# A small GpSimd copy ahead of the first weight load is taken out of a fused attention and feed-forward kernel

## The chip, the cores and the metric

The kernel runs on one core of one Trainium2 chip. The metric is device time in microseconds (us) of one execution, the median of several runs. Before the change it is 179.35 us (three runs, 179.14 to 179.39).

## What is computed

A gated linear recurrence over 768 positions, for 4 batches of 8 heads with head size 48, and behind it a two-layer network on all 3072 rows of 384 numbers:

```python
f = 1.0 / (1.0 + np.exp(-f_logit))
for t in range(S):
    state = f[:, :, t, :, None] * state + np.einsum('bhd,bhe->bhde', k[:, :, t], v[:, :, t])
    y[:, :, t] = np.einsum('bhd,bhde->bhe', q[:, :, t], state)
...
h = x @ w_in                      # 384 -> 2048
out = np.maximum(0.01 * h, h) @ w_out   # 2048 -> 384
```

All inputs and the output are float32.

## The kernel before

**Tiles.** The work is cut into twelve pairs, m = 0 to 11: pair m belongs to batch m % 4 and holds 2 x 128 positions of all 8 heads. The first four pairs are thus the first 256 positions of the four batches. For each pair four loads of 384 KB bring the gate input F, the keys K, the queries Q and the values V into float32 tiles `RAW["F"]`, `RAW["K"]`, `RAW["Q"]` and `RAW["V"]`, which have three slots each. Below, F1 means F of pair 1, the second pair, and so on. F1 goes to slot 1, F2, K2, Q2 and V2 to slot 2.

**A pair's way.** ScalarE takes exp(-F) and then ln(1 + .), which is minus the logarithm of the gate; a product with a triangular matrix on TensorE sums it along the positions; ScalarE turns the sums into decay factors; VectorE or GpSimd multiply K and Q with them (`scale`, L294). `state_pe` (L354) forms the pair's contribution to the state, `turn_pe` (L310) transposes the scaled K and Q, `score` (L324) multiplies them, `mask` (L333) masks, `mix` (L342, L345) forms y. `y_out`, `x_pe` (L381) and `x_out` move y, transposed, to `XT`. Then `up` (L392) multiplies with w_in, 8 groups of 6 matmuls for a pair; `up_act` (L408) is the leaky ReLU; `down` (L420) multiplies with w_out; `put` and `out_pair` bring the rows out. The first two pairs go through shorter code of the same kind with names that begin with `f_`.

**The weights.** w_in and w_out are float32 in memory and bf16 in their tiles. `load_w_in(0)` and `load_w_in(1)` (L246) bring one half each, 768 KB as stored in the tile; `up` groups 0 to 3 need the first half, groups 4 to 7 the second. Four `load_w_out` (L249) bring a quarter each. All six are issued by GpSimd and go through the queue q0; the loads of F, K, Q and V are issued by SyncE (L255) and go through q1. Both queues are served by the same 16 DMA engines.

**The order.** The whole program is one list written out by hand. Each engine does its part of the list in that order, and waits at the first instruction whose inputs aren't there; what stands behind it waits too. Around the change the list reads, cut to what matters (slot numbers are the last arguments of `load`):

```python
v_cast(G, 0, 0)            # GpSimd: V of pair 0 to bf16
load('F', 2, 2)            # SyncE
f_exp(1)                   # ScalarE: exp of F1, in place
touch('F', 1)              # GpSimd
load_w_in(0)               # GpSimd issues
load('V', 2, 2)            # SyncE
load_w_in(1)               # GpSimd issues
load('K', 2, 2)            # SyncE
v_cast(G, 1, 1)            # GpSimd: V of pair 1 to bf16
load_w_out(0, 1)           # GpSimd issues
put_state(0, 0)            # GpSimd
load('Q', 2, 2)            # SyncE
```

`touch` (L242) copies the last column of a slot of a raw tile to a tile `seen` of 128 x 1 that nothing reads. On ScalarE, `gate_exp(2)` (L259), the exp of F2, stands ahead of `x_out(A, 0, 0)` (L127), which gives the first `XT`, and ahead of `gate_ln(2)` (L262) and the first `up_act`. On VectorE, `v_cast(V, 2, 2)` of V2 stands ahead of `scale(V, 0, 2, 0, 1)` of K2 and `scale(V, 1, 2, 0, 1)` of Q2; `state_pe(1, 2, 1, 5)` on TensorE waits for the first two, `turn_pe(1, 1, 2)` for the third.

Of the kernel before, what the change touches and what calls it, by code (L numbers as in the profile page):

```python
# [15 lines left out]
def kernel(  # L16
# [122 lines left out]
    def f_exp(s, hh=None):  # L139
        t = part("F", s)[:, hd(hh)]  # L140
        A.activation(t, t, AF.Exp, scale=-1.0)  # L141
# [99 lines left out]
    def touch(name, s):  # L241
        G.tensor_copy(out=seen, in_=RAW[name][:, s, 96 * H - 1:96 * H])  # L242

    def load_w_in(x):
        c = 512 * sum(WP[:x])
        G.dma_start(out=WI[x], in_=moe_w_in.rearrange("(a p) n -> p a n", p=128)[:, :, c:c + 512 * WP[x]])  # L246
# [234 lines left out]
    f_back(0, 0, 5)  # L481
    v_turn(0, 6, 6 + 1)
    f_exp(1)
    touch('F', 1)
    load_w_in(0)
    idle_pe(1, 1)
    f_back_out(V, 0, 5)
# [753 lines left out]
```

## Time and profile before

| | |
|---|---|
| median of three runs | 179.35 us (179.14 to 179.39) |
| the profiled execution's own time | 179.37 us |
| span of its instructions | 177.7 us |
| TensorE busy | 167.7 us (94%) |
| ScalarE, VectorE, GpSimd busy | 114.0, 107.8, 70.8 us |
| granted TensorE clock | 0.999 |
| moved by DMA | 31.68 MB |

The span runs from the first to the last instruction of one profiled execution; 1.67 us of its time lie outside the span. In the profile PE is TensorE's matmuls, PEld its weight loads, DVE is VectorE, ACT ScalarE, POOL GpSimd, and SPq the queue of SyncE, which only issues transfers. In a timeline a row gives the start, the length, the engine, the line, the operation, out<-in, the shape and the count, and in brackets how long the engine had been idle and what ended that. A DMA row there is its issue and not the transfer; the time from issue to landing stands in other views. In the DMA view the rows of a queue give packets, megabytes, and the time that the packets took as a share of the 16 engines' time in that stretch, which can be above 100% since packets overlap.

### The profile page before, as it was taken

The numbers are of one execution on the slowest core, as the hardware profiler recorded it, in microseconds if no ns is written. First come the engines' busy times: TensorE is split into PE (matmuls) and PEld (weight loads), VectorE is DVE, ScalarE is ACT, GpSimd is POOL, SyncE is SP. The second block draws the span as 40 slices with busy tenths as digits, with TensorE's granted clock in tenths as the row PEclk, the third lists the DMA queues.
The fourth block names the chain that finished last, engine by engine and source line by source line (L and its number), as shares of the span: only waits on it lengthen the run. The fifth ranks groups of instructions, "written<-read, shape, count | busy, mean of one in ns | idle before, by whom it ended". The sixth has DMA issues, their size and how long they took to land.

```text
span 177.7 us, 4589 instructions
## 1 busy us (share of the span) xinstructions
PE 167.7 (94%) x1850; PEld 134.6 (76%) x1850; DVE 107.8 (61%) x219; ACT 114.0 (64%) x196; POOL 70.8 (40%) x114
## 2 busy tenths in 40 slices
PE   6987689999999999999999999999999999999992
PEld 4655579876795888697698688697796978778871
DVE  5298955357899996587979999393861302030110
ACT  3979459499589759779479598259162835336520
POOL 7369420037955540593666395756320000000000
PEclk9999999999999999999999999999999999999999
DMA  5999999999989999989999679988484000021315
GB/s 141 322 325 246 210 214 214 282 270 300 283 232 285 278 311 292 184 199 274 173 268 137 150 182 202 156 151 167 79 149 95 0 0 4 0 61 32 89 44 133
DMA packets 73764, 31.68 MB, mean 178 GB/s; under 512 B 69264, under 2 KB 72464, under 8 KB 73744
## 3 DMA queue, kind: packets, MB, share of 16 engines
q1 hardware_dynamic: 71680, 27.96, 67.1%
q0 software_dynamic: 1376, 3.15, 9.2%
q10 hardware_dynamic: 688, 0.30, 0.6%
q8 instruction: 14, 0.23, 0.5%
q14 instruction: 6, 0.05, 0.1%
HBM read 25.17 MB, written 4.72 MB: 168 GB/s over the span
## 4 chain that ended last, share of the span: by engine, by line
PE 81%; DMA 10%; SPq 3%; DVE 2%; ACT 1%; POOL 1%; issue 0%
PE ps L420 34%; PE ps L392 33%; DMA w_in<-in_moe_w_in_dram 7%; PE ps L324 3%; DMA rawF<-in_f_logit_dram 3%; SPq L255 2%; PE ps L345 2%; PE ps L354 2%; PE ps L342 2%; PE ps L425 1%; PE ps L310 1%; PE ps L381 1%; DVE kh L294 1%; PE ps L268 1%; POOL w_in L246 0%; ACT rawF L141 0%
## 5 line engine op out<-in xcount | busy, mean ns | idle before, releaser
L408 ACT ACTIVATE gT<-ps 128x512 bf16<-128x512 f32 x96 | 56.1, 599 | 33.0 <-PE ps L392 29.8
L392 PE MATMUL ps<-xT,w_in 128*128 128x256 bf16 x576 | 67.4, 273 | 2.2 <-DMA w_in<-in_moe_w_in_dram 2.2
L420 PE MATMUL ps<-w_out,gT 128*128 128x384 bf16 x368 | 65.9, 326 | 0.0
L392 PEld LDWEIGHTS <-w_in 128*128 128x128 bf16 x576 | 61.7, 113 | 3.6 <-DMA w_in<-in_moe_w_in_dram 2.4
L420 PEld LDWEIGHTS <-gT 128*128 128x128 bf16 x368 | 34.2, 98 | 20.2 <-issue 0.2
L333 DVE TENSOR_TENSOR wm<-ps,mask 128x512 bf16<-128x512 f32 x40 | 25.5, 684 | 9.7 <-PE ps L324 6.7
L129 DVE COPY osb<-ps 128x384 f32<-128x384 f32 x13 | 7.2, 555 | 29.6 <-PE ps L420 19.9
L236 POOL CAST sb<-sf 64x192 bf16<-64x192 f32 x40 | 15.3, 383 | 22.4 <-DVE sf L231 14.2
L302 DVE COPY vb<-vq 64x384 bf16<-64x384 bf16 x40 | 14.9, 372 | 1.0 <-PE ps L345 0.3
L361 DVE TENSOR_TENSOR sf<-sf,ps 64x192 f32<-64x192 f32 x32 | 11.2, 348 | 5.8 <-PE ps L354 4.8
L364 POOL TENSOR_TENSOR sf<-sf,aend 128x192 f32<-128x192 f32 x14 | 7.6, 542 | 13.7 <-DVE sf L361 12.4
L294 POOL TENSOR_TENSOR kh<-rawQ,aa 128x384 bf16<-128x384 f32 x12 | 11.7, 995 | 1.4 <-ACT aa L288 1.2
L294 DVE TENSOR_TENSOR kh<-rawK,em 128x384 bf16<-128x384 f32 x16 | 10.9, 721 | 1.7 <-DMA rawK<-in_k_dram 1.6
L127 ACT COPY osb<-ps 128x384 f32<-128x384 f32 (+1 forms) x12 | 5.3, 456 | 9.9 <-PE ps L420 6.8
L129 POOL CAST vq<-rawV 128x768 bf16<-128x768 f32 x10 | 8.9, 900 | 5.3 <-DMA rawV<-in_v_dram 5.3
L265 POOL TENSOR_TENSOR ls<-rawF 128x384 bf16<-128x384 f32 x8 | 8.5, 1068 | 6.1 <-ACT rawF L262 3.6
L127 ACT CAST xn<-ps 128x384 bf16<-128x384 f32 x15 | 7.1, 478 | 5.5 <-PE ps L345 5.4
L133 PE MATMUL ps<-fill 128*128 128x256 bf16 x38 | 7.9, 350 | 1.4 <-DVE fill L102 1.4
L285 ACT ACTIVATE em<-rawF 128x768 bf16<-128x768 f32 x10 | 8.5, 849 | 0.8 <-POOL rawF L279 0.6
L345 PE MATMUL ps<-vb,wm 128*128 128x48 bf16 x192 | 8.7, 183 | 0.0
L262 ACT ACTIVATE rawF<-rawF 128x768 f32<-128x768 f32 x10 | 8.4, 842 | 0.1
L259 ACT ACTIVATE rawF<-rawF 128x768 f32<-128x768 f32 x10 | 8.5, 846 | 0.0
(81 smaller groups left out, 175.6 us busy)
## 6 DMA issues: line engine op xcount, KB each, us to landing
rawK<-in_k_dram SPq DMA_DIRECT2D x12, 384.0 KB, 5.3
rawQ<-in_q_dram SPq DMA_DIRECT2D x12, 384.0 KB, 5.1
rawV<-in_v_dram SPq DMA_DIRECT2D x12, 384.0 KB, 5.0
rawF<-in_f_logit_dram SPq DMA_DIRECT2D x11, 384.0 KB, 5.0
out_dram<-osb SPq DMA_DIRECT2D x22, 192.0 KB, 3.1
w_in<-in_moe_w_in_dram POOLq DMA_DIRECT2D x2, 768.0 KB, 11.0
w_out<-in_moe_w_out_dram POOLq DMA_DIRECT2D x4, 384.0 KB, 14.7
kT<-kh SPq DMA_TRANSPOSE x14, 4.5
```

The source lines that it names most:

```text
L127: eng.copy(out=out, in_=in_)
L129: eng.tensor_copy(out=out, in_=in_)
L236: G.tensor_copy(out=SB[r, b, s, :, e * D:(e + 1) * D], in_=SF[r, b])
L259: A.activation(RAW["F"][:, s], RAW["F"][:, s], AF.Exp, scale=-1.0)
L294: eng.tensor_mul(o[:, :, j, :, 0:D], x[:, :, j], y[:, :, j])
L302: V.tensor_copy(out=VB[64 * j:64 * j + 64, vb, w, :], in_=VQ[64 * w:64 * w + 64, t, j * KD:(j + 1) * KD])
L333: V.tensor_mul(WM[:, wm, c].rearrange("p (i n) -> p i n", n=128), bank(bk)[:, c].rearrange("p (i n) -> p i n", n=128), masks(4 if hh is No ...
L345: nc.tensor.matmul(bank(bk)[:, h * D:(h + 1) * D], WM[:, wms[h % 2], 128 * (h // 2):128 * (h // 2) + 128], VB[:, vb, w, h * D:(h + 1) * D] ...
L361: V.tensor_add(SF[r, b], SF[r, b], pt[r, :, e * D:(e + 1) * D])
L392: nc.tensor.matmul(bank(bk)[:, i * 256:(i + 1) * 256].rearrange("p (w n) -> p w n", w=2), WQ[g // 2][:, f, :, g % 2 * 2 + i], XT[:, t, :, ...
L408: A.activation(GT[:, t, 2 * g:2 * g + 2, :].rearrange("p f n -> p (f n)"), bank(bk), AF.Prelu, alpha=0.01)
L420: nc.tensor.matmul(bank(bk)[:, 0:KD], GT[:, t, ff, 128 * w:128 * w + 128], WO[:, ff, :], start=(ff == 0), stop=(ff == NF - 1))
```

## The change

One line of the list goes; nothing else is edited.

```diff
     f_back(0, 0, 5)
     v_turn(0, 6, 6 + 1)
     f_exp(1)
-    touch('F', 1)
     load_w_in(0)
     idle_pe(1, 1)
```

On GpSimd, this is the place of the copy in the program as built, with the semaphores that each instruction waits for: DMAHW5 tells of the landing of V0, DMAHW6 of that of F1, and Activation counts ScalarE's instructions, here its exp of F1.

```order
 L129 CAST kh_71<-rawK_65 128x8x48 [waits DMAHW3_49]
 L129 CAST vq_72<-rawV_67 128x768 [waits DMAHW5_49]
-L242 COPY seen_117<-rawF_64 128x1 [waits DMAHW6_49,Activation_49]
 L246 DMA w_in0_83<-in_moe_w_in_dram 128x3x1024
 L246 DMA w_in1_84<-in_moe_w_in_dram 128x3x1024
```

The two loads wait for nothing of their own in either program, so they now stand right behind the cast of V0.

On SyncE, the later loads of F, K, Q and V have the same order, and some of their waits on a slot's earlier readers are written down elsewhere (Pool counts GpSimd's instructions). The rows are F3, F4, F5, K3, K4, Q3 and V3 in this order.

```order
 L255 DMA rawF_64<-in_f_logit_dram 128x8x96 [waits DMAHW5_49,Activation_49]
-L255 DMA rawF_64<-in_f_logit_dram 128x8x96 [waits DMAHW6_49,Activation_49,Pool_49]
+L255 DMA rawF_64<-in_f_logit_dram 128x8x96 [waits DMAHW6_49,Activation_49]
 L255 DMA rawF_64<-in_f_logit_dram 128x8x96 [waits DMAHW1_49,DMAHW7_49,DVE_49,Activation_49]
-L255 DMA rawK_65<-in_k_dram 128x8x96 [waits DMAHW0_49]
-L255 DMA rawK_65<-in_k_dram 128x8x96
+L255 DMA rawK_65<-in_k_dram 128x8x96 [waits DMAHW0_49,Pool_49]
+L255 DMA rawK_65<-in_k_dram 128x8x96 [waits Pool_49]
 L255 DMA rawQ_66<-in_q_dram 128x8x96 [waits DMAHW2_49]
-L255 DMA rawV_67<-in_v_dram 128x8x96 [waits DMAHW3_49]
+L255 DMA rawV_67<-in_v_dram 128x8x96 [waits DMAHW3_49,Pool_49]
```

F4's load no longer waits for the copy, and K3's, K4's and V3's now name the GpSimd casts that read their slots before, which the wait for the copy had covered. In the same way the first `f_state_pool` on GpSimd (L225) now names ScalarE beside VectorE.

## The prediction

> **What bounds the kernel now.** I read the chain of waits first, in shares and then in order of time:
>
> ```profile
> PE 81%; DMA 10%; SPq 3%; DVE 2%; ACT 1%; POOL 1%; issue 0%
> ...
> 10.36 0.85 ACT rawF L141
> ...
> 11.46 0.87 POOL w_in L246
> 12.33 12.79 DMA w_in<-in_moe_w_in_dram
> ...
> 25.16 1.50 PE ps L392 x12
> ```
>
> The end is set by TensorE, but the chain enters TensorE at 25.16 us, through the landing of the second half of w_in at 12.33 + 12.79 = 25.12. Behind that the table of stages (its length, then the busy time of PE, PEld, DVE, ACT and POOL, each with its instructions, the granted clock, the DMA share and GB/s) shows no room on TensorE: it is busy in 19.52 of the 20 us from 40 and in all of those from 60.
>
> ```profile
> 40.00:60.00 20.00, 19.52 (x252) 14.95 (x250) 17.67 (x35) 15.97 (x29) 14.74 (x21) 1.00 1.03 278
> 60.00:80.00 20.00, 20.00 (x211) 16.27 (x210) 16.09 (x33) 15.06 (x27) 9.18 (x14) 1.00 0.99 247
> ```
>
> So what TensorE wins at 25.16 it keeps, unless something else comes late. The timeline of TensorE shows what it waits for before:
>
> ```profile
> 18.83 0.51 PE L215 MATMUL ps<-vb,kb 128*128 128x96 bf16 x8
> 20.75 1.50 PE L392 MATMUL ps<-xT,w_in 128*128 128x256 bf16 x12 [1.41 <-DMA w_in<-in_moe_w_in_dram]
> ...
> 25.16 1.50 PE L392 MATMUL ps<-xT,w_in 128*128 128x256 bf16 x12 [0.75 <-DMA w_in<-in_moe_w_in_dram]
> ...
> 36.08 0.51 PE L354 MATMUL ps<-vq,kh 64*128 64x96 bf16 x16
> ```
>
> It is idle 1.41 us before the first half and 0.75 before the second, 2.16 in all. From the start of `up` 0 it needs 25.16 - 0.75 - 20.75 = 3.66 us to reach `up` 4. GpSimd's timeline says why w_in is late:
>
> ```profile
> 9.19 0.83 POOL L129 CAST vq<-rawV 128x768 bf16<-128x768 f32 x1 [1.71 <-DMA rawV<-in_v_dram]
> 11.27 0.19 POOL L242 COPY seen<-rawF 128x1 f32<-128x1 f32 x1 [1.25 <-ACT rawF L141]
> 11.39 1.72 POOL L246 DMA_DIRECT2D w_in<-in_moe_w_in_dram  x2
> 13.12 1.04 POOL L129 CAST vq<-rawV 128x768 bf16<-128x768 f32 x1
> ```
>
> The copy takes 0.19 us, and GpSimd stands idle 1.25 us ahead of it for the exp of F1.
>
> **What goes, and what moves.** The cast of V0 ends at 10.02. A load was issued about 0.05 us before the end of the instruction ahead of it (11.39 against 11.46 at the copy), so the first issue comes at about 9.97 instead of 11.39: 1.42 us sooner. The second issue, the cast of V1, the w_out loads and `put_state` follow in line; none of them waits in the rows above, V1 landing before 13.12 at the latest. If the cast of V1 waits for V1, only w_out behind it feels that.
>
> The waits that are written differently cost nothing: the GpSimd casts which K3, K4 and V3 now name end by 14.16 and those loads are issued far later, and the exp that `f_state_pool` now names is ahead of it by several us.
>
> **What the sooner load does to the other queue.** The DMA view in four stretches, 12.34 to 14.39, 14.39 to 15.0, 15.0 to 16.4 and 16.4 to 29 us (queue: packets, MB, share):
>
> ```profile
> q1 hardware_dynamic: 1705, 0.65, 113.5%
> ...
> q0 software_dynamic: 40, 0.08, 70.7%
> q1 hardware_dynamic: 238, 0.09, 56.1%
> ...
> q0 software_dynamic: 132, 0.27, 102.2%
> q1 hardware_dynamic: 72, 0.03, 8.8%
> ...
> q0 software_dynamic: 1001, 2.27, 93.6%
> q1 hardware_dynamic: 997, 0.38, 16.9%
> ```
>
> In the first stretch q0 has no packet: w_in's transfer begins at 14.39, 3.00 us behind its issue. Until then q1 moves 1705 packets in 2.05 us, 832 per us. Then it still moves 238 in 0.61 us and 72 in 1.4 us, and from there 997 in 12.6 us, 79 per us: the engines take one packet of each queue in turn, and q0's are larger. Whatever SyncE has in its queue when w_in starts is starved. These are its issues, and behind them the times to landing of F2, V2, K2, Q2 and F3, and of both halves of w_in:
>
> ```profile
> 9.08 1.11 SPq L255 DMA_DIRECT2D rawF<-in_f_logit_dram  x1
> 10.24 1.33 SPq L255 DMA_DIRECT2D rawV<-in_v_dram  x1
> 11.61 1.15 SPq L255 DMA_DIRECT2D rawK<-in_k_dram  x1
> 12.80 2.42 SPq L255 DMA_DIRECT2D rawQ<-in_q_dram  x1
> 15.34 19.07 SPq L255 DMA_DIRECT2D rawF<-in_f_logit_dram  x3
> ...
> rawF<-in_f_logit_dram SPq DMA_DIRECT2D x1, 384.0 KB, 4.9
> ...
> rawV<-in_v_dram SPq DMA_DIRECT2D x1, 384.0 KB, 6.2
> ...
> rawK<-in_k_dram SPq DMA_DIRECT2D x1, 384.0 KB, 19.1
> ...
> rawQ<-in_q_dram SPq DMA_DIRECT2D x1, 384.0 KB, 21.7
> ...
> rawF<-in_f_logit_dram SPq DMA_DIRECT2D x1, 384.0 KB, 20.3
> ...
> DMA to landing us min/median/max: 9.3/11.0/12.8
> ```
>
> F2 lands at 13.98, V2 at 16.44, K2 at 30.7, Q2 at 34.5, F3 at 35.6. A load is 384 KB in packets of 384 bytes, 1024 of them. V2 landed within 238 + 72 = 310 packets of w_in's start, so at 14.39 at least 714 were through, which at 832 per us took 0.86 us: F2's data had ended by 13.53, about 0.45 before its landing.
>
> **The estimate of F2.** With the same 3.00 us, w_in's transfer now starts at 9.97 + 3.00 = 12.97. Then (13.53 - 12.97) x 832 = 466 packets of F2 are left. 310 of them go in the 2.0 us that such a start gives, 156 at 79 per us take 2.0 more: data until 16.97, landing at 17.4. (From below: it could keep its 13.98 if the start were 0.56 us later; from above it is 18.3, if the landing lags by 1.3 us, an estimate from K2, which landed at 30.7 where 1024 packets at 79 per us behind 16.4 make 29.4.) Who waits for F2 is ScalarE, and behind it in order everything else there:
>
> ```profile
> 16.45 0.89 ACT L259 ACTIVATE rawF<-rawF 128x768 f32<-128x768 f32 x1
> 18.14 0.80 ACT L127 COPY xT<-ps 128x768 bf16<-128x768 bf16 x1 [0.80 <-PE ps L381]
> 18.84 0.85 ACT L262 ACTIVATE rawF<-rawF 128x768 f32<-128x768 f32 x1
> ...
> 36.68 0.83 ACT L259 ACTIVATE rawF<-rawF 128x768 f32<-128x768 f32 x1
> ```
>
> The exp then runs 17.4 to 18.3 instead of 16.45 to 17.34, and `x_out` to 19.1 instead of 18.94. The first half of w_in now lands at 9.97 + 9.3 = 19.3, and TensorE is free at 19.34. So `up` 0 starts at about 19.4, and even at F2's upper end at 20.0 (18.3 + 0.89 + 0.80). `up` 4 is then reached at 23.1 to 23.7, while the second half lands at 25.12 - 1.42 = 23.70. **F2's delay is hidden behind w_in**, and would begin to show where F2 lands behind 18.4.
>
> **V2, K2, Q2 and F3.** Both queues hold the same bytes, so what is last in q1 ends when it did: Q2 stays near 34.5 and F3 near 35.6. V2 comes behind F2 at 79 per us, 13 us later, at 30.4 or so; K2, 1.2 us of full rate ahead of Q2, at about 33.3. VectorE wants them in order:
>
> ```profile
> 27.51 0.55 DVE L129 CAST vq<-rawV 128x768 bf16<-128x768 f32 x1
> ...
> 30.76 1.03 DVE L294 TENSOR_TENSOR kh<-rawK,em 128x384 bf16<-128x384 f32 x2 [1.61 <-DMA rawK<-in_k_dram]
> 34.51 1.03 DVE L294 TENSOR_TENSOR kh<-rawQ,aa 128x384 bf16<-128x384 f32 x2 [2.72 <-DMA rawQ<-in_q_dram]
> ```
>
> The cast waits to 30.4, the scaling of K2 ends at 34.3 instead of 31.8. `state_pe`, which needs it, would now be reached at 36.08 - 1.42 = 34.66: 0.3 us to spare, where there were 4.3. The exp of F3 would be reached at 35.26 and waits to 35.6 or 35.7, some 0.4 us on ScalarE, of which I let 0.1 through to TensorE.
>
> **The sum.** Removed at `up` 4: 1.42. Given back: F2 0 (0 to 0.1), K2 0 (0 to 0.9, were it as late as Q2), F3 0.1 (0 to 0.4). That leaves 1.3 of the profiled execution's 179.37 us, which is within 0.02 of the median: **178.1**. The gain can't be much over 1.42, since w_in itself moves no further.
>
> **Rivals.** A difference under 0.2%, 0.36 us, can't be told from no change by measuring this kernel.
>
> *F2 starved, slower.* In the estimate everything hangs on when w_in's first packet comes. Each 0.1 us sooner leaves 83 packets more, 1.05 us at 79 per us. `up` 4 stays at 25.16 if `up` 0 starts at 21.5, so if F2 lands at 19.8, so at a start of 12.73: only a quarter of a microsecond before mine. A start at 12.5 leaves 857 packets, 6.9 us at 79 per us behind the first 2.0: landing at 21.9, `up` 0 at 23.5, `up` 4 at 27.2, 2.0 us late: 181.4. For it: the 3.00 us were measured once, on engines that q1 had filled. Against it: they are as full 1.4 us sooner, and GpSimd does the same sequence behind. Chance 0.21.
>
> *A first packet sooner still.* If of the 3.00 us a part was waiting that an earlier issue doesn't have, and I take a third, the packet comes 2.00 us behind the issue, at 11.97. Then 1298 packets of Q1 and F2 are left, (1298 - 310) / 79 = 12.5 us: F2 at 26.9, `up` 0 at 28.6, `up` 4 at 32.3, 7 us late: 186.5. Chance 0.05, since the only start in the trace speaks for 3.00. The Trainium skill (DMA: Bandwidth & Descriptors, Specifications) gives a first-byte latency of about 1 us for transfers issued by GpSimd; the issue itself takes about 0.9 us, so by that page the start would lie near this rival. This case's trace has 3.00.
>
> *K2 or F3 take most of it.* If the loads that are pushed back land as late as Q2, `state_pe` starts 0.9 late and 0.5 is left: 178.9. For it, 0.3 us to spare; against it, the queue's order. Chance 0.11, of which 0.04 under the 0.36.
>
> *No change.* The start at 14.39 follows the end of F2's data and not the issue, as if q0 had to wait for q1 to make room; then w_in lands as before: 179.4. Against it, V2 was already running then. Chance 0.10.
>
> **How the numbers follow.** My forecast has 0.53. Faster is 0.53 + 0.07 = 0.60, the same 0.10 + 0.04 = 0.14, slower 0.21 + 0.05 = 0.26. The forecast's own range is 177.8 to 178.5; to hold 8 in 10 the range goes on over the two middle cases, 0.74 so far, to 180.3, the milder half of the starved case.
>
> **What would show it.** In the profile after: GpSimd issues w_in at about 10.0; the first q0 packet at 13.0; `gate_exp(2)` waits for F2 until about 17.4; `up` 0 at 19.4 and `up` 4 at 23.75; the cast of V2 on VectorE waits until about 30.4, the scaling of K2 until 33.3; everything on TensorE from 25 on some 1.3 sooner. It is wrong if F2 lands behind 19.8, or if `state_pe` at 34.7 waits for more than a microsecond.

## The result, and the profile after

The changed kernel takes **178.00 us** (median of 20 executions, 177.73 to 180.84) beside 179.39 us before (20 executions, 179.04 to 180.19). The ratio is 0.9936, with a 95% interval of 0.9917 to 0.9954: faster by 1.39 us, of 1.3 forecast. The profiled execution took 177.88 us, with a span of 176.2 where it was 177.7. Five of the 20 executions lie above 178.5, at 178.63 to 180.84; the last section comes back to them. All ratios here leave out executions that lie far above the others of their kernel; the times given with them are medians of all, so a ratio is not the quotient of two of these times.

The chain of waits in order of time, of the changed kernel:

```profile
4.29 4.81 DMA rawV<-in_v_dram
9.10 0.05 issue
9.15 0.83 POOL vq L129
9.98 0.87 POOL w_in L246
10.85 12.77 DMA w_in<-in_moe_w_in_dram
23.62 0.05 issue
23.67 1.50 PE ps L392 x12
```

The exp of F1 on ScalarE is gone from the chain. Ahead of the issue of w_in now stands the cast of V0, and ahead of that V0's own transfer. From the end of its issue to its landing w_in takes as long as before (12.77 and 12.79 us), so it lands sooner by what the issue is sooner. GpSimd's timeline shows by how much:

```profile
9.15 0.83 POOL L129 CAST vq<-rawV 128x768 bf16<-128x768 f32 x1 [1.70 <-DMA rawV<-in_v_dram]
9.92 1.72 POOL L246 DMA_DIRECT2D w_in<-in_moe_w_in_dram  x2
11.64 0.84 POOL L129 CAST vq<-rawV 128x768 bf16<-128x768 f32 x1
```

The first issue comes at 9.92, 1.47 us sooner, and the cast of V1 behind it waits for nothing. TensorE's timeline, at the places shown of before:

```profile
18.45 0.51 PE L215 MATMUL ps<-vb,kb 128*128 128x96 bf16 x8
19.26 1.50 PE L392 MATMUL ps<-xT,w_in 128*128 128x256 bf16 x12 [0.29 <-DMA w_in<-in_moe_w_in_dram]
...
23.67 1.50 PE L392 MATMUL ps<-xT,w_in 128*128 128x256 bf16 x12 [0.76 <-DMA w_in<-in_moe_w_in_dram]
...
34.59 0.51 PE L354 MATMUL ps<-vq,kh 64*128 64x96 bf16 x16
```

`up` 4 starts 1.49 us sooner than before and `state_pe` at 34.59 also 1.49 sooner, without a wait; the span is 1.5 shorter. So nothing was given back on the way. The wait before `up` 0 fell from 1.41 to 0.29, the one before `up` 4 stayed (0.75, 0.76).

What the sooner transfer did to the other queue is in the timelines of ScalarE and VectorE:

```profile
16.42 0.89 ACT L259 ACTIVATE rawF<-rawF 128x768 f32<-128x768 f32 x1
17.76 0.80 ACT L127 COPY xT<-ps 128x768 bf16<-128x768 bf16 x1 [0.46 <-PE ps L381]
...
35.59 0.84 ACT L259 ACTIVATE rawF<-rawF 128x768 f32<-128x768 f32 x1 [0.30 <-DMA rawF<-in_f_logit_dram]
...
30.02 0.56 DVE L129 CAST vq<-rawV 128x768 bf16<-128x768 f32 x1 [3.92 <-DMA rawV<-in_v_dram]
...
33.20 1.03 DVE L294 TENSOR_TENSOR kh<-rawK,em 128x384 bf16<-128x384 f32 x2 [1.52 <-DMA rawK<-in_k_dram]
34.39 1.03 DVE L294 TENSOR_TENSOR kh<-rawQ,aa 128x384 bf16<-128x384 f32 x2 [0.16 <-DMA rawQ<-in_q_dram]
```

V2 was pushed back from 16.43 to 29.99 and K2 from 30.67 to 33.10, while Q2 (34.36, before 34.48) and F3 (35.57, before 35.69) stayed. The scaling of K2 ends at 34.23, 0.36 ahead of `state_pe`. F2 was not pushed back at all: its exp starts at 16.42, without a wait.

The DMA view from the issue of w_in to its first packet, and of the 0.64 us behind that:

```profile
q1 hardware_dynamic: 2773, 1.05, 116.8%
...
q0 software_dynamic: 43, 0.09, 73.6%
q1 hardware_dynamic: 246, 0.09, 50.9%
```

From 9.92 to 13.16 only q1 moves, 2773 packets in 3.24 us. With w_in's first packet at 13.16, q1 still gets 246 packets through in 0.64 us. These were the last of F2, which landed at 13.94.

### The profile page after: what moved, and what is told of

It reads as the page before. It is cut to its first block, busy times and chain, and to the rows that moved or that the text cites. A ratio compares the mean times of both kernels' runs of the same rounds, so it can differ in the third digit from the quotient of the medians.

```text
span 176.2 us, 4589 instructions
## 1 busy us (share of the span) xinstructions
PE 167.3 (95%) x1850; PEld 134.1 (76%) x1850; DVE 107.1 (61%) x219; ACT 113.9 (65%) x196; POOL 70.5 (40%) x113
## 4 chain that ended last, share of the span: by engine, by line
PE 82%; DMA 10%; DVE 2%; SPq 2%; POOL 1%; ACT 1%; issue 0%
PE ps L420 34%; PE ps L392 34%; DMA w_in<-in_moe_w_in_dram 7%; PE ps L324 3%; DMA rawV<-in_v_dram 3%; PE ps L345 2%; PE ps L354 2%; PE ps L342 2%; SPq L255 2%; PE ps L425 2%; PE ps L310 1%; PE ps L381 1%; DVE kh L294 1%; PE ps L268 1%; POOL w_in L246 0%; POOL vq L129 0%
## 5 line engine op out<-in xcount | busy, mean ns | idle before, releaser
L302 DVE COPY vb<-vq 64x384 bf16<-64x384 bf16 x40 | 13.5, 336 | 1.0 <-PE ps L345 0.3
L294 DVE TENSOR_TENSOR kh<-rawK,em 128x384 bf16<-128x384 f32 x16 | 11.5, 760 | 1.6 <-DMA rawK<-in_k_dram 1.5
```

The costliest lines, as they stand in the source:

```text
L294: eng.tensor_mul(o[:, :, j, :, 0:D], x[:, :, j], y[:, :, j])
L302: V.tensor_copy(out=VB[64 * j:64 * j + 64, vb, w, :], in_=VQ[64 * w:64 * w + 64, t, j * KD:(j + 1) * KD])
```

## The experiments

All kernels are the changed one but for the edit shown, except where the text says that it starts from another. Ratios are against before, measured on the same chip with each group.

**The copy without its wait.** The copy is put back, but from F0, whose exp is long done.

```diff
     f_exp(1)
+    touch('F', 0)
     load_w_in(0)
```

> The copy stays in its place, but reads F of pair 0, whose exp has long ended, so that nothing is waited for. Theory (w_in follows its issue, and the wait for the exp of F1 was what held it): first issue of w_in at about 10.1, 0.2 later than without the copy, up 4 at 23.85, 178.2 us. Rival (the copy itself, or an instruction of that kind ahead of the load, costs the time): 179.3 us as before.

It took 178.04 us (4 executions, 177.81 to 178.31), ratio 0.9938 (0.9919 to 0.9956). TensorE's timeline:

```profile
19.68 1.50 PE L392 MATMUL ps<-xT,w_in 128*128 128x256 bf16 x12 [0.44 <-DMA w_in<-in_moe_w_in_dram]
24.08 1.50 PE L392 MATMUL ps<-xT,w_in 128*128 128x256 bf16 x12 [0.74 <-DMA w_in<-in_moe_w_in_dram]
```

w_in is issued at 10.12, 0.20 later than without the copy, and `up` 4 starts 0.41 later, yet 1.08 sooner than before. The wait for the exp of F1 was what the old line cost; the 0.19 us of the copy itself can't be told apart in the time.

**Only the second half late.** The old copy, with its wait, stands between the two loads.

```diff
     load_w_in(0)
...
     score(1, 0, 4, 4 + 1)
+    touch('F', 1)
     load_w_in(1)
```

> The copy and its wait stand between the two loads of w_in, so the first half is issued at 9.9 and the second at 11.5. Theory (one queue, the second half's data begin only when the first's have ended at 17.8): the second half lands at 23.6 as after the change, 178.0 to 178.2 us. Rival (each half follows its own issue): the second half lands at 25.1, up 4 starts at 25.2, 179.4 us.

178.10 us (4 executions, 177.87 to 178.12 and one of 185.47), ratio 0.9933 (0.9909 to 0.9958). The halves were issued at 10.09 and 11.52 and landed at 19.39 and 23.81; `up` 4 started at 23.86. The second half lay in line behind the first, so its own issue, 0.67 later than in the changed kernel, doesn't set its landing. What counts is the first issue.

**Sooner by a quarter of a microsecond.** Half of the cast of V0 goes to ScalarE, so that GpSimd is done with its half sooner.

```diff
-    v_cast(G, 0, 0)
+    v_cast_half(G, 0, 0, 0)
+    v_cast_half(A, 0, 0, 1)
```

> After the change, with the cast of V0 split in two halves, one on GpSimd and one on ScalarE: w_in is issued another 0.4 sooner, at about 9.5, its first packet comes at about 12.75 instead of 13.17. Theory (what SyncE has in its queue at the first packet is starved, and F2 is next): F2 lands between 17 and 19.5 instead of 13.9, its exp waits for it, up 0 starts between 19.3 and 21, up 4 between 23.3 and 24.6; 177.7 to 178.9 us, not the further 0.4 of gain. Rival (F2 gets through whatever the start is): F2 at 13.9, up 4 at 23.3, 177.6 us.

177.85 us (4 executions, 177.81 to 177.96), ratio 0.9928 (0.9912 to 0.9943). w_in is issued at 9.65. Now F2 is starved: it lands at 17.82. ScalarE's and TensorE's timelines:

```profile
17.84 0.84 ACT L259 ACTIVATE rawF<-rawF 128x768 f32<-128x768 f32 x1 [1.23 <-DMA rawF<-in_f_logit_dram]
...
19.42 0.33 PE L215 MATMUL ps<-vb,kb 128*128 128x96 bf16 x4 [0.61 <-ACT xT L127]
23.64 1.50 PE L395 MATMUL ps<-xT,w_in 128*128 128x256 bf16 x12 [0.42 <-DMA w_in<-in_moe_w_in_dram]
```

ScalarE waits 1.23 us for F2, and the wait reaches TensorE as 0.61 at 19.42. It ends there: `up` 4 starts at 23.64, when the second half has landed (23.59), as in the changed kernel. F2's landing is close to the 17.4 that the prediction had worked out, though not by that working (see the section on why it was right), and it costs nothing.

**Much sooner.** The first load goes ahead of the cast of V0.

```diff
     idle_pe(2, 7)
+    load_w_in(0)
     v_cast(G, 0, 0)
...
     f_exp(1)
-    load_w_in(0)
     idle_pe(1, 1)
```

> After the change, with the first half of w_in issued ahead of the cast of V0, at about 7.5 to 7.6, so its first packet comes at about 10.8. Theory (starved queue): Q1 and F2 are hit, Q1 lands at about 25 instead of 12.7 and F2 about 30; everything of pair 1 and the first x_out waits; 186 to 193 us. Rival (no starvation that matters): w_in no longer bounds the start, 177 to 178 us.

Two executions, 186.25 and 191.92 us, with 179.14 for before. w_in is issued at 7.72 and its first packet comes at 10.69, while V1 is being moved; V1 lands at 19.60, Q1 at 21.88, F2 at 23.09. TensorE's timeline:

```profile
22.47 1.03 PE L176 MATMUL ps<-ident,kh 128*128 128x128 bf16 x8 [8.29 <-ACT kh L127]
```

It waits 8.29 us for a cast of Q1, which waits for the load. The rival's mechanism is real: a load in q1 that is in line when w_in starts is starved, and TensorE can be made to wait for it.

**Where the edge lies.** The cast of V0 goes to ScalarE. In its place on GpSimd stands a memset of a part of `GT`, which is written before it is read; its length sets when w_in is issued.

```diff
-    v_cast(G, 0, 0)
+    G.memset(GT[:, 0, 0:7, :], 0.0)
+    v_cast(A, 0, 0)
```

With 7 of `GT`'s blocks; the two kernels after it have `0:8` and `0:9`.

> After the change, with the cast of V0 on ScalarE and a memset on GpSimd in its place, so that w_in is issued at about 9.1 and its first packet comes at about 12.2 to 12.5. Theory (F2 is starved once w_in starts well before F2's data end at 13.5): F2 lands at 22 to 25, up 0 starts at 24 to 27, 182 to 186 us. Rival (the hidden delay grows no further than in the halved cast): 177.5 to 178 us.

> The same with the issue at about 9.25. Theory: first packet at 12.1 to 12.7, F2 at 20 to 29, 182 to 190 us. Rival: about 178 us.

> As with the issue at 9.0, but with a longer memset, so w_in is issued at about 9.45. Theory (a cliff: once w_in's first packet comes well before F2's data end, F2 is starved; the first packet comes 1.9 to 2.5 us behind the end of the issue while SyncE's queue is full, so at 12.3 to 12.9): F2 lands at 18 to 28, 178 to 189 us, and executions differ by microseconds. Rival (a smooth cost, of 0.1 us of time per 0.1 us of issue): about 178 us.

The issues came at 9.02, 9.10 and 9.33. With 7 blocks: 190.1 us (2 executions), ratio 1.0603 (1.0572 to 1.0633), F2 at 28.97. With 8: 187.94 (4 executions, 187.88 to 188.53), ratio 1.0480 (1.0462 to 1.0498), F2 at 26.91. With 9: executions of 179.53, 179.95, 180.48, 181.59, 183.93, 188.56 and 190.40 us, ratio 1.0055 (1.0024 to 1.0086), F2 at 21.91 in the profiled one of 183.93. TensorE's timeline with 7 blocks, and its table of stages (PE, PEld, DVE, ACT, POOL, granted clock, DMA share, GB/s):

```profile
30.57 0.48 PE L215 MATMUL ps<-vb,kb 128*128 128x96 bf16 x4 [9.17 <-ACT xT L127]
```

```profile
26.00:28.00 2.00, 0.00 (x0) 0.00 (x0) 0.00 (x0) 0.00 (x0) 0.00 (x0) 0.50 1.09 213
28.00:30.00 2.00, 0.00 (x0) 0.00 (x0) 0.00 (x0) 1.01 (x2) 0.00 (x0) 0.50 1.06 225
30.00:32.00 2.00, 1.43 (x10) 1.12 (x10) 0.00 (x0) 1.26 (x2) 0.60 (x1) 0.50 1.16 320
32.00:34.00 2.00, 2.00 (x18) 1.51 (x17) 0.74 (x3) 0.95 (x2) 1.47 (x4) 0.50 1.14 307
```

And with 9 blocks:

```profile
23.51 0.48 PE L215 MATMUL ps<-vb,kb 128*128 128x96 bf16 x4 [3.58 <-ACT xT L127]
```

The wait is that for `x_out`, which stands behind the exp of F2 on ScalarE: 9.17 us and 3.58. With an issue only 0.6 us sooner than in the changed kernel, none of the seven executions with 9 blocks is below the median of before (179.35), and they lie up to 11 us apart. For 7 blocks I had expected F2 at 22 to 25 and a smaller loss: the mechanism was right, its size too small. The cast on ScalarE has a price too (the first half of L215 starts at 19.54 and 19.59 with 8 and 9 blocks, beside 18.45); it lies ahead of these waits and wasn't measured alone. By an estimate from these rows, L215 (0.51 us) and the 3.66 us from `up` 0 to `up` 4 behind 19.59 put `up` 4 at about 23.8, 0.1 behind the changed kernel, so the wait for F2 is by far the larger part. With 7 blocks L215 starts at 21.06, since Q1 too is late there: it lands at 15.76, beside 12.74.

**Later, on the safe side.** A memset of two blocks ahead of the first load.

```diff
     f_exp(1)
+    G.memset(GT[:, 0, 0:2, :], 0.0)
     load_w_in(0)
```

> After the change, with a memset of about 0.45 us between the cast of V0 and the load of w_in, so w_in is issued at about 10.4. Theory: F2 is through before w_in starts, with more to spare; w_in, up 4 and the end come at most 0.45 later than after the change, 178.0 to 178.5 us, and no execution lies far above the others.

177.96 us (5 executions, 177.86 to 178.32), ratio 0.9920 (0.9907 to 0.9934). The DMA view of this kernel, from the issue at 10.59 to 13.30, and the 0.6 us behind that:

```profile
q1 hardware_dynamic: 2327, 0.88, 117.0%
...
q0 software_dynamic: 34, 0.07, 74.7%
q1 hardware_dynamic: 203, 0.07, 44.6%
```

w_in is issued 0.67 us later than in the changed kernel, and its first packet comes only 0.14 later, 2.71 us behind the issue. F2 lands at 14.27. `up` 4 starts at 24.11 in the profiled execution, the slowest of the five, 0.44 later than in the changed kernel's; by the medians the time is that of the changed kernel.

**The loads behind w_in held back.** V2, K2 and Q2 are issued by SyncE only once a memset on VectorE has written V2's slot, at 18.2 us, when q1 has nothing else left.

```diff
     f_back_out(V, 0, 5)
-    load('V', 2, 2)
...
     f_ln(1, 0, 0)
-    load('K', 2, 2)
...
     f_turn(1, None, 2, 2)
-    load('Q', 2, 2)
...
     f_back_out(V, 2, 7)
+    V.memset(RAW['V'][:, 2, 96 * H - 1:96 * H], 0.0)
+    load('V', 2, 2)
+    load('K', 2, 2)
+    load('Q', 2, 2)
```

> After the change, with the loads of V2, K2 and Q2 held on SyncE until about 18, by a one-column memset of V2's slot on VectorE ahead of them. Theory (the two queues take turns, so w_in is slowed by what is starved): w_in has the engines alone until about 19, its halves land about 0.3 and 0.7 sooner, up 4 at 23.0; K2 and F3 now close behind, so 177.3 us, 0.7 below the change, at least 0.3. Rival (w_in goes at its own rate, whatever runs beside it): halves land as after, 178.0, or later if K2 comes late.

177.37 us (5 executions, 177.28 to 177.95), ratio 0.9901 (0.9885 to 0.9916): **the lowest median of all kernels here**. The changed kernel was run again in the same group:

> The changed kernel once more, beside the others of this group. Both theories: 178.0 us. If F2 wins its race with w_in by a hair, as the one profile has it (data until 13.6, first packet of w_in at 13.2), some executions lie 0.5 us and more above the median, as 5 of the 20 did; if those were chance, hardly any does.

178.14 us (5 executions of 177.75 to 178.31 and one of 191.35), ratio 0.9930 (0.9916 to 0.9944). The DMA view from 14 to 19 us, of the changed kernel run again:

```profile
q0 software_dynamic: 444, 0.88, 94.2%
q1 hardware_dynamic: 330, 0.13, 14.5%
```

The same stretch with the loads held:

```profile
q0 software_dynamic: 525, 1.04, 111.7%
```

Alone, q0 moves 1.04 MB where it moved 0.88 beside q1, and the halves land at 18.70 and 22.35 instead of 19.18 and 23.71. `up` 0 and `up` 4 no longer wait, and `up` 4 starts 1.35 us sooner than in the changed kernel run again (22.40 and 23.75). What is late next, on TensorE with the loads held:

```profile
33.64 0.22 PE L354 MATMUL ps<-vq,kh 64*128 64x96 bf16 x2 [0.25 <-DVE kh L294]
34.11 0.47 PE L354 MATMUL ps<-vq,kh 64*128 64x96 bf16 x14 [0.25 <-DVE kh L294]
...
39.59 0.62 PE L324 MATMUL ps<-kT 64*128 64x128 bf16 x16 [0.49 <-ACT kT L127]
```

These are 0.99 us: `state_pe` waits for the scaling of K2, and a `score` for ScalarE, which had waited 0.96 for F3 and 1.09 for F4. By the profiled execution, the slowest of its five, 0.36 is left, and its span is 0.2 shorter; by the medians it is 0.77, by the ratios 0.5, and the two intervals only touch.

**The same hold, in the kernel before.** The edit is the same, with the copy and its wait in place.

> The kernel before, copy and wait in place, with the same hold on V2, K2 and Q2. Theory: w_in starts at 14.4 as before and runs alone, its halves land 0.3 and 0.7 sooner than 20.7 and 25.1, up 4 at 24.5; 178.7 us. Rival: 179.4 as before.

179.17 us (12 executions, 178.71 to 179.62), ratio 0.9992 (0.9980 to 1.0004): no change, where 178.7 was expected. The DMA view from the issue at 11.41 to 13.30, then of the 0.6 us behind that:

```profile
q1 hardware_dynamic: 1615, 0.61, 116.7%
...
q0 software_dynamic: 16, 0.03, 77.5%
q1 hardware_dynamic: 118, 0.04, 25.3%
```

w_in's first packet comes 1.89 us behind the issue, as q1 runs dry, and not 3.00. The halves land at 19.13 and 23.00 and `up` 4 starts at 23.05, 2.1 us sooner than before and sooner than in the changed kernel. Most of it is lost at `state_pe`, as the timelines of TensorE and VectorE show:

```profile
34.95 0.22 PE L354 MATMUL ps<-vq,kh 64*128 64x96 bf16 x2 [0.92 <-DVE kh L294]
35.42 0.47 PE L354 MATMUL ps<-vq,kh 64*128 64x96 bf16 x14 [0.25 <-DVE kh L294]
...
32.65 0.56 DVE L129 CAST vq<-rawV 128x768 bf16<-128x768 f32 x1 [7.17 <-DMA rawV<-in_v_dram]
```

V2 lands at 32.63 (31.31 with the hold in the changed kernel), K2 at 33.81, F3 at 36.27. Behind `state_pe` TensorE is only 0.70 us ahead of before (35.89 and 36.59). It is 0.16 ahead at `down` at 96.41, which waits 0.29 for ScalarE, and ScalarE had waited 1.10 there for a later load of F. This is the rival "K2 or F3 take most of it", in another kernel. It also shows that a sooner `up` 4 is worth little where q1's loads end late.

**w_out moved behind them.** This starts from the changed kernel with the loads held. To keep the 1.35 us, the last two loads of w_out go behind `decay_em(2, 0)`, with a copy on GpSimd that waits for it.

```diff
     state_dve(0, 6)
-    load_w_out(2, 1)
     v_turn(1, 4, 4 + 1)
     mix(1, 0, (0, 0), [2, 2 + 1], 0, 7)
-    load_w_out(3, 1)
...
     decay_em(2, 0)
+    G.tensor_copy(out=seen, in_=EM[:, 0, 96 * H - 1:96 * H])
+    load_w_out(2, 1)
+    load_w_out(3, 1)
```

> The loads held as before in the version with 177.4 us, and the last two quarters of w_out issued only behind the decay factors of pair 2 (a one-column GpSimd copy of them stands ahead), at about 27 instead of 14.3 and 14.8. Theory (the held version is bound by V2, K2, F3 and F4, which wait behind w_out's packets): V2 and K2 land 3 us and more sooner, state_pe no longer waits, F3 and F4 about as before; 176.9 us, at least 0.2 below the held version. Rival (the bytes are the same, so what is won by K2 is lost by F3, F4 or by w_out itself): 177.4 us or more.

179.57 us (12 executions, 177.4 to 186.54), ratio 0.9966 (0.9937 to 0.9994): worse than the hold alone. V2, K2, Q2 and F3 do land sooner, at 27.57, 28.77, 30.00 and 31.15, but the timelines of TensorE and ScalarE, from an execution of 180.51 us, show other waits:

```profile
34.89 0.81 PE L420 MATMUL ps<-w_out,gT 128*128 128x384 bf16 x4 [0.38 <-DMA w_out<-in_moe_w_out_dram]
37.05 1.28 PE L420 MATMUL ps<-w_out,gT 128*128 128x384 bf16 x4 [1.34 <-DMA w_out<-in_moe_w_out_dram]
...
37.92 0.84 ACT L259 ACTIVATE rawF<-rawF 128x768 f32<-128x768 f32 x1 [2.17 <-DMA rawF<-in_f_logit_dram]
```

w_out is wanted at 35, and its last two quarters land at 34.85 and 37.00 (28.73 and 30.79 with the hold alone). F4, which is now the load in line beside them, is issued 3.8 us sooner than with the hold alone and still lands no sooner (37.90 and 37.77). The forecast of a gain was wrong: the bytes are the same and the wait moved. What spreads the executions over 9 us was not looked into.

## Why the prediction was right, step by step

**The gain.** Right in place and size. The issue came 1.47 us sooner (1.42 forecast), both halves landed 1.49 sooner, and TensorE had it all at `up` 4. `copy_no_wait` and `second_half_late` show that it is the wait ahead of the first issue. The size has some luck in it: w_in's first packet came only 1.23 sooner (14.39 and 13.16), and from there to the landing of the second half it took 10.46 us where it had taken 10.72. Why that stretch was shorter wasn't looked into.

**The first packet "with the same 3.00 us".** This step does not hold, though it came out 0.19 off. The fourteen traces have 1.89 to 3.50 us, and what is steady is the place in q1. Counting q1's packets of 384 bytes up to q0's first, in loads of 1024 (F0's half on this queue is the first 0.5, so that F2 is 7.5 to 8.5):

```
kernel              issue  first packet  loads moved  F2 landed  time, us
w_in_ahead_of_cast   7.72     10.69         6.13        23.09    186 to 192
issue_9_1            9.02     11.88         7.20        28.97    190
issue_9_2            9.10     11.92         7.34        26.91    188
issue_9_5            9.33     12.49         7.80        21.91    180 to 190
cast_halved          9.65     13.15         8.26        17.82    177.9
the changed kernel   9.92     13.16         8.28        13.94    178.0
after_again          9.98     13.17         8.31        13.99    178.1
copy_no_wait        10.12     13.20         8.34        14.25    178.0
issue_10_4          10.59     13.30         8.32        14.27    178.0
before              11.39     14.39         9.23        13.97    179.4
```

Issues from 9.65 to 10.59 all give a first packet at 13.15 to 13.30 (three more kernels of the study with issues between, 9.96 to 10.09, have 13.14 to 13.32). The packet comes near the end of a load in q1, with 0.16 to 0.37 of it left in all rows but that of `issue_9_5`. So it is a staircase with steps of one load, some 1024 packets at 832 per us, 1.23 us: from 14.39 to 13.16 is one step.

The packets of the traces show where a step ends. A load in q1 closes with 16 packets of 4 bytes, one for each of its 16 parts. In eleven of the fourteen traces w_in's first packet starts within 0.01 us behind one of them, the first, second or third of its load: so w_in gets in where a part of q1's load is through. `issue_9_1`, `issue_9_5` and `w_in_ahead_of_cast` are the exceptions, with 0.05 to 0.15 us to the nearest of them. `before_loads_held` shows the step by experiment: with V2 taken out of q1, w_in's first packet comes at the end of F2 (13.30) and no longer at the end of V2 (14.39), for an issue at the same time. What decides which load's end it is stays open.

**F2 at 17.4.** Wrong for the changed kernel: it landed at 13.94. The packet came at 13.16 instead of 12.97, and 228 packets of F2 were left then, not 466; q1 moved all of them within 0.64 us. (In the trace of before F2's last part ended at 13.64, where the working had its data through by 13.53.) In `cast_halved`, with the packet at 13.15, F2 lands at 17.82, close to the number forecast, but that is luck. 248 packets were left, fewer than the 310 that the working lets through at once, so by it F2 would not have been held up. In the trace 15 of F2's 16 parts have ended by 14.09, with 230 packets of q1 through by 14.1; at least 18 of the last part are left then, and it ends at 17.48. One part of the sixteen was starved, and the landing waits for the last. That such a landing hides behind w_in was the step that the forecast rested on, and that run shows it.

**V2, K2, Q2, F3.** Right: 29.99 (30.4 or so forecast), 33.10 (33.3), 34.36 (34.5), 35.57 (35.6). The rate of 79 packets per us beside w_in, and the same bytes in both queues, were enough.

**What is given back.** The 0.1 for F3 was too much: ScalarE waited 0.30 and TensorE nothing. That term, and the issue 0.05 sooner than forecast, are the small miss in the sum.

**The rivals.** *F2 starved* is the other side of a real edge. It was put at a first packet of 12.73, and 181.4 us at 12.5; with one at 12.49 the executions run from 179.5 to 190.4, and at 11.9 from 188 to 191. The edge lies between issues of 9.33 and 9.65 (the kernels on its two sides also differ in where V0 is cast), so the changed kernel stands 0.3 to 0.6 us from it. *A first packet sooner still* is half true: at least 1.1 of the 3.00 was waiting in line, as `before_loads_held` shows with 1.89, which is 0.94 us behind the end of the issue (12.36 to 13.30), when q1 runs dry. The Trainium skill (DMA: Bandwidth & Descriptors, Specifications) gives about 1 us to the first byte for such transfers. Counted from the end of the issue, that trace agrees with its 0.94; the thirteen others do not, with 1.8 to 2.6. *K2 or F3* did not come here, with 0.36 us to spare, and came where V2 landed later. *No change* was wrong in its time; that the start follows q1 and not the issue was the better half of it.

## What to carry to other kernels

Where two queues share the DMA engines, ask of a sooner transfer which loads of the other queue are in line when its first packet comes, and how long each can wait; here V2 could be 13.6 us late at no cost and F2 3.9 us, while an issue 0.8 us sooner still cost 10 us. Measure a start at several issue times before calling it a latency. Holding back small loads that nobody wants yet gave 0.5 to 0.8 us on top of the change, until the next load in line was the late one.

## What the runs showed that was not expected

The start of w_in's transfer in steps of one load of the other queue, above: an issue later by 0.67 us (`issue_10_4`) moved it by 0.14.

Two queues at once cost little beyond their bytes: from 14 to 19 us q0 and q1 moved 0.88 + 0.13 = 1.01 MB together, and q0 alone 1.04; from 15 to 18 us it was 0.51 + 0.10 in the changed kernel and 0.61 with the loads held. What the hold gave w_in is the share that q1 had taken.

The long waits of TensorE came with a lower clock. With `issue_9_1` the granted clock is 0.50 from 26 to 34 us, in the wait of 9.17 us and on behind it, and a matmul of `up` takes 421 ns there (273 in the changed kernel). `w_in_ahead_of_cast`, with its wait of 8.29 us, has 0.50 from 18 to 26.

Single executions of the changed kernel lie far above the others: the five above 178.5 in the first 20, and one of 191.35 (granted clock 0.964, as in the 190.66 us execution of `issue_9_1`) in the six of `after_again`; of before, none of 64 is above 180.75. With F2's edge so close this would fit a start on the wrong side of it, but no trace of such an execution was taken, so that is only argued. The five executions of `issue_10_4`, with more room to that edge, have none above 178.32; five are few.
